# Retention and a gated feed-forward: the fourth block with one key a partition and a DMA transpose

## The chip, the cores and the metric

The kernel runs on one core of a Trainium2 chip. The core has five engines: TensorE (PE in the profile) for matmuls, VectorE (DVE), ScalarE (ACT), GpSimd (POOL), and SyncE (SP), which here only issues DMAs. 16 DMA engines move data between HBM and SBUF, the on-chip memory of 128 partitions; PSUM is the small memory into which TensorE writes. The metric is the device time of one execution in microseconds. Three executions of the kernel before took 296.79, 297.09 and 298.65 us, a median of 297.09. One more was profiled.

## What is computed

The first half is retention, attention without a softmax, with a decay that depends on the head. The second half is a feed-forward layer with the activation h cos(h). q, k and v have 8 batches, 8 heads, 576 positions and 64 columns; in x, the result of the first half, they are 4608 tokens of 512 columns.

```python
scores = q @ k.transpose(0, 1, 3, 2) / sqrt(64)
gamma = 1 - 2.0 ** (-5 - arange(8))                 # one for each head
D = where(rel >= 0, gamma ** rel, 0)                # rel = query position - key position
x = (scores * D) @ v                                # then heads side by side: 4608 x 512
h = x @ w_in                                        # 512 -> 2048
out = (h * cos(h)) @ w_out                          # 2048 -> 512
```

## The kernel before

**Blocks and tiles.** The tokens are cut into 18 blocks of 256 tokens, each of two chunks of 128. Two blocks make a tile of 512 tokens, and there are nine tiles, `n` = 0 to 8. Retention runs by blocks, the feed-forward by tiles, and the blocks of later tiles are worked on between the feed-forward matmuls of the present one.

**A block.** Its steps and their names are as follows.
- `load` brings q, k and v by DMA into float32 tiles `fq`, `fk`, `fv`, three buffers each. The issues stand on the SP queue.
- `scaled` multiplies q and k by powers of gamma that depend on the position and writes them as bf16 into `qks`; `prep` does all four parts on GpSimd. `round_v` casts v into `vb`.
- The transposed q and k, `qkT`, come either from TensorE (`transpose_pe`, with a copy from PSUM) or from one DMA transpose (`transpose_dma`, on the SP queue, named DMA_TRANSPOSE in the profile).
- `scores` multiplies keys and queries inside a chunk into `sc`; VectorE multiplies by a mask into `ret`.
- `sums_of` adds up k times v, the state (`st`), that is carried to later chunks.
- `outputs` adds the chunk's own part (`out_own`, line 375) and the carried part (`out_carried`, line 407) into `ov`, and the result is copied into `xT`.

`qks`, `vb` and `qkT` have four buffers each.

**Two layouts.** A block below `NP_B` (4 before) is in the pair layout: a partition holds two neighbouring keys, 512 contiguous bytes in HBM, and each chunk has half of the partitions. From `NP_B` on, a partition holds one key (two loads each for k and v, in pieces of 256 B), and the state sums and the chunk's own outputs take half the matmuls. q always has two rows a partition. Blocks 0 to 3 are transposed by TensorE, blocks 4 to 17 by DMA.

**The feed-forward.** `mm1` multiplies `xT` by `w_in`; ScalarE takes the cosine (line 457) and VectorE multiplies (line 460) into `gT`. The second matmul of tile 0 is direct (line 927). From tile 1 on `mm2_seven` forms it from seven products (line 563, named x = 1 to 7) of sums of operands, as in Strassen's scheme. The operand sums on the token side (`g_sum`, line 503, tiles `gs3`, `gs5`, `gs6`, `gs7`) are split between VectorE and GpSimd: GpSimd forms gs3 in tile 1 and gs7 in later tiles, four operations each.

**The order.** Nothing is rearranged: each engine executes its instructions in the order of the program text. On the SP queue each DMA is issued behind the one ahead of it, and an issue that must wait holds all that follow. `step` puts `prep`, the DMA transpose and `round_v` of the next block, and a load, in the queues; `steps_to` does so until a given block. In tile 1 the step of block 4 follows the first group of `mm1`, those of 5 and 6 the second, the one of 7 comes behind one of the tile's stores, and the one of 8 in tile 2 behind the seventh group of `mm1`. The scores of block 8 stand in tile 2 inside `mm2_seven`, ahead of product x = 3 (`end_unit`, line 994).

Of the kernel before, what the change touches and what calls it, by code (L numbers as in the profile page):

```python
# [13 lines left out]
ALU = mybir.AluOpType  # L14
# [3 lines left out]
def kernel(  # L18
# [9 lines left out]
    nc = tc.nc  # L28
    P = 128
    B, H, S, D = q.shape  # L30
    assert (B, H, S, D) == (8, 8, 576, 64)
    HG = H // 2
# [14 lines left out]
    last = NT - 1  # L47
    BK = 256
    NB = NTOK // BK
    NP_B = 4  # L50
    PERQ = 9
    PERK = 9
    MIX = PERK // 2
# [131 lines left out]
        tiles["vb", j] = vb  # L185

    def prep(j):
        for name in "kq" if j < NP_B else "qk":
            for y in range(2):
                scaled(nc.gpsimd, j, name, y)  # L190

# [37 lines left out]
    def scores(j, banks):  # L229
        cs = chunks[j]  # L230
        kT = tiles["qkT", j]
        ret = retp.tile([P, 2, HG, 2, P], BF16, tag="ret", name="ret")
        pss = [
            psum.tile([P, HG, 2, P], F32, tag=t, name="sc")
            if isinstance(t, str)
            else [psum.tile([P, HG, P], F32, tag=u, name="sc") for u in t]
            for t in banks
        ]
        if cs[0].pair:
            order = [(c, y, he, hg) for hg in range(HG) for y in range(2) for he in range(2) for c in cs]  # L240
            mask = mask_mix if any(c.mixed for c in cs) else mask_p
            for c, y, he, hg in order:
                ps = pss[he]
                nc.tensor.matmul(
                    ps[y][c.rows, hg, :] if isinstance(ps, list) else ps[c.rows, hg, y, :],
                    lhsT=kT[he * D : he * D + D, 1, y, hg, c.rows],
                    rhs=q_cols(c, he, hg),
                    start=True,
                    stop=True,
                )  # L250

            def masked(he):
                if isinstance(pss[he], list):
                    for y in range(2):
                        nc.vector.tensor_tensor(
                            out=ret[:, he, :, y, :],
                            in0=pss[he][y],
                            in1=mask[:, y].unsqueeze(1).to_broadcast([P, HG, P]),
                            op=ALU.mult,
                        )  # L260
                    return
                nc.vector.tensor_tensor(
                    out=ret[:, he].rearrange("p b r i -> p b (r i)"),
                    in0=pss[he].rearrange("p b r i -> p b (r i)"),
                    in1=mask.rearrange("p r i -> p (r i)").unsqueeze(1).to_broadcast(
                        [P, HG, 2 * P]
                    ),
                    op=ALU.mult,
                )
        else:  # L270
            ret = ret.rearrange("p a b r i -> p (a b r i)").rearrange(
                "p (k a b i) -> p k a b i", k=2, a=2, b=HG
            )
            pss = [
                ps.rearrange("p b r i -> p (b r i)").rearrange("p (a b i) -> p a b i", a=2, b=HG)
                for ps in pss
            ]
            for c in cs:
                for hg in range(HG):
                    for i0 in range(0, P, HP):  # L280
                        for he in range(2):
                            nc.tensor.matmul(  # L282
                                pss[c.k][i0 : i0 + HP, he, hg, :],
                                lhsT=kT[he * D : he * D + D, 1, c.k, hg, i0 : i0 + HP],
                                rhs=q_cols(c, he, hg),
                                start=True,
                                stop=True,
                            )

            def masked(k):  # L290
                mask = mask_cmix if cs[k].mixed else mask_c
                nc.vector.tensor_tensor(  # L292
                    out=ret[:, k].rearrange("p a b i -> p (a b) i"),
                    in0=pss[k].rearrange("p a b i -> p (a b) i"),
                    in1=mask.unsqueeze(1).to_broadcast([P, H, P]),
                    op=ALU.mult,
                )

        tiles["ret", j] = ret
        return [lambda: masked(0), lambda: masked(1)]  # L300
# [213 lines left out]
    def sums_after(n, i):  # L514
        if n == 1:
            slots = {5: ((5, 0, 4),), 6: ((6, 0, 4),)}
        else:
            slots = {
                2: ((7, 0, 4),),
                3: ((5, 0, 4),),  # L520
                4: ((6, 0, 4), (7, 4, 6)),
                5: ((3, 0, 4),),
                6: ((5, 4, 6), (7, 6, E2)),
            }
        for x in slots.get(i, ()):
            g_sum(n, *x)
# [46 lines left out]
    def stored_rows(r0, c0, c1, t, queues=(nc.sync, nc.sync)):  # L573

        rows = out[r0 : r0 + P * t.shape[1], c0:c1].rearrange(
            "(j i r) c -> r i j c", r=2, i=HP
        )
        for r in range(2):
            queues[r].dma_start(rows[r], t[r * HP : (r + 1) * HP])
# [85 lines left out]
    def load_next(**kw):  # L665
        nonlocal loaded
        if loaded < NB:
            load(loaded, **kw)
            loaded += 1
# [143 lines left out]
    w_dma.append(load_w_out(12))  # L813
    scaled(nc.gpsimd, 2, "q", 0)
    load_next(names="kqv", gate=w_dma[6])
    load_next()
    prepared = 4

    def intro(j, sc_banks, st_bank, put_off=None, then=None):
        add = sums_of(j, st_bank)  # L820
# [41 lines left out]

    stores = []

    for n in range(NT):
        blocks = blocks_of.get(n) or [(e + k * E2, 0, W) for e in range(0, E2, 2) for k in range(2)]
        for i, (et, c0, cw) in enumerate(blocks):
            inside = {
                (0, 1): {2: block1_carried},
                (1, 0): {2: lambda: transpose_pe(3, "q", "b", act)},  # L870
                (1, 2): {3: block3_scores},
                (1, 3): {2: lambda: sums_of(3, "st")()()},
            }.get((n, i), {})
            off = [] if (n, i) == (1, 3) else None
            between = block1_sums if (n, i) == (0, 0) else None
            mm1(n, et, c0, cw, banks_of.get(n, "abmabmab")[i], inside, off, between)
            if (n, i) == (0, 0):
                block1_own()
            if (n, i) == (1, 0):
                step(False)  # L880
                load_next()
                for r0, ot in stores:
                    stored_rows(r0, 0, DM, ot)
            if (n, i) == (1, 1):
                step(False)
                load_next()
                step()
            if (n, i) == (1, 3):
                mm2_seven(1, {}, None, (1,), lambda: (outputs(3, "m"), off.pop()()))
            if n:  # L890
                sums_after(n, i)
            if (n, i) == (2, 6):
                step()
        if n == 0:
            gT = tiles["g", n]
            two = psum.tile([P, 2, DM], F32, tag="m", name="o")
# [6 lines left out]
                (37, lambda: round_v(2)),  # L903
                (42, block2_scores),
                (50, block2_sums),
                (50, lambda: prep(3)),
                (57, load_next),
                (59, lambda: round_v(3, (act, act))),
                (60, lambda: outputs(2, "b")),
                (62, lambda: transpose_pe(3, "k", "a", act)),  # L910
            ]
            todo += [
                (at, lambda x=x, e=e: w_sums(x, e, e + 4))
# [10 lines left out]
            for done, (t, e) in enumerate(order):  # L924
                while todo and todo[0][0] <= done:
                    todo.pop(0)[1]()
                nc.tensor.matmul(  # L927
                    pss[t],
                    lhsT=gT[:, e, t * P : (t + 1) * P],
                    rhs=w_out_sb[:, e, :],  # L930
                    start=(e == 0),
                    stop=(e == ET - 1),
                )
                for u in range(2 * (t == 1) if t < 2 else 1) if e == ET - 1 else ():
                    u = u if t < 2 else t
                    ot = op.tile([P, 1, DM], F32, tag="abcd"[u], name="ot")
                    (act, vec)[u % 2](ot[:, 0], pss[u])
                    stores.append((u * P, ot))
            continue

        a, b = 2 * n + 2, 2 * n + 3
# [23 lines left out]
        def first_scores(flush, pend):  # L965
            g_sum(n, 5, 4, E2)
            g_sum(n, 6, 4, E2)
            masks = scores(a, "ab")
            add_a = sums_of(a, "st")
            add_b = sums_of(b, "m")  # L970
            masks[0]()
            add_a()()
            masks[1]()
            g_sum(n, 3, 0, E2)
            g_sum(n, 7, 0, 4)
            tiles["rounded"] = add_b()
            g_sum(n, 7, 4, E2)

        def next_scores(flush, pend):
            outputs(a, "a")  # L980
# [30 lines left out]

        def stored(u):
            if n == 1:
                steps_to({2: 8}.get(u, 0))
            else:
                steps_to({0: 2 * n + 6, 3: 2 * n + 7}.get(u, 0))

# [31 lines left out]
```

## Time and profile before

| | us |
|---|---|
| median of three executions | 297.09 |
| the profiled execution | 296.28 |
| its span, first to last instruction | 294.6 |
| busy: TensorE | 283.2 |
| busy: VectorE | 215.6 |
| busy: GpSimd | 145.6 |
| busy: ScalarE | 143.0 |

The profile is of one execution. Its span is 1.7 us shorter than its device time. Times in the views count from the start of the span. "Busy" is the time in which an engine had an instruction running; waits are given beside it as idle time and what ended it. The chain is followed backwards from the last instruction: at each step to what released it, or to the instruction ahead of it on its engine. An issue on the SP queue (SPq) lasts as long as the queue needs to hand the DMA over, not until the data has landed. The granted clock was 0.994 of full speed on the whole, and below 1 only in the first 12 us.

### The profile page before, as it was taken

To read this page: it belongs to the slowest core of one execution; us is meant where nothing else is said; L and a number is where in the kernel's file an instruction comes from. 1 tells how busy PE (TensorE), PEld (TensorE's weight loads), DVE (VectorE), ACT (ScalarE), POOL (GpSimd) and SP (SyncE) were. 2 spreads that over 40 slices of the span, in tenths; PEclk is the share of its full clock that TensorE was granted. 3 is DMA by queue.
4 is the path that set the end of the run, shared out by engine and by line. 5 is a ranking of instruction groups with operands and counts; after the bars stand their busy time and mean duration, and the time that the engine had idled before them with its cause. 6 is when DMAs were issued, how large, how long until landed. Compare 5 with 4: busy or idle time off the path is not lost.

```text
span 294.6 us, 7623 instructions
## 1 busy us (share of the span) xinstructions
PE 283.2 (96%) x3248; PEld 195.0 (66%) x3268; DVE 215.6 (73%) x268; ACT 143.0 (49%) x166; POOL 145.6 (49%) x172
## 2 busy tenths in 40 slices
PE   7889999999999999999999999999999999999993
PEld 2568755878864688458845884588458845874583
DVE  4585748558986999699659965996599659835933
ACT  4466537646436624563356335633563356326620
POOL 8641535847864495839713961497148014102400
PEclk9799999999999999999999999999999999999999
DMA  7999999999899999999999999979930630121014
GB/s 197 268 222 215 232 247 214 231 181 231 198 199 227 204 240 210 191 219 197 236 203 193 243 215 197 219 128 223 203 64 21 127 71 0 38 65 44 2 37 107
DMA packets 128930, 49.78 MB, mean 169 GB/s; under 512 B 89344, under 2 KB 128384, under 8 KB 128896
## 3 DMA queue, kind: packets, MB, share of 16 engines
q1 hardware_dynamic: 124288, 44.84, 75.6%
q0 software_dynamic: 4224, 4.19, 8.8%
q8 instruction: 25, 0.41, 0.6%
q10 hardware_dynamic: 384, 0.26, 0.4%
q14 instruction: 9, 0.07, 0.1%
HBM read 36.70 MB, written 9.44 MB: 157 GB/s over the span
## 4 chain that ended last, share of the span: by engine, by line
PE 79%; DVE 10%; DMA 4%; POOL 2%; ACT 2%; issue 1%; DVEq 0%; ACTq 0%
PE h L445 38%; PE o L563 27%; PE o L927 5%; DVE gT L460 3%; PE ov L375 3%; DVE gs L503 3%; DMA qkT<-qks 2%; PE st L319 2%; POOL qks L167 2%; PE sc L282 2%; DVE ret L292 2%; PE ov L407 1%; DMA fk<-in_k_dram 1%; PE tr L210 1%; ACT cosh L457 1%
## 5 line engine op out<-in xcount | busy, mean ns | idle before, releaser
L445 PE MATMUL h<-xT,w_in_sb 128*128 128x512 bf16 (+1 forms) x690 | 126.6, 340 | 1.0
L460 DVE TENSOR_TENSOR gT<-h,cosh 128x1024 bf16<-128x1024 f32 x72 | 87.9, 1221 | 37.5 <-ACT cosh L457 37.4
L457 ACT ACTIVATE cosh<-h,half_pi 128x1024 f32<-128x1024 f32 x72 | 80.2, 1114 | 66.4 <-PE h L445 65.1
L445 PEld LDWEIGHTS <-w_in_sb 128*128 128x128 bf16 x704 | 68.4, 98 | 55.3 <-issue 0.6
L503 POOL TENSOR_TENSOR gs<-gT 128x512 bf16<-128x512 bf16 x28 | 35.8, 1280 | 92.2 <-DVE gT L460 92.2
L563 PEld LDWEIGHTS <-gs 128*128 128x128 bf16 x528 | 49.5, 98 | 6.4
L167 POOL TENSOR_TENSOR qks<-fq,gq 128x512 bf16<-128x512 f32 x31 | 33.9, 1113 | 18.1 <-DMA fq<-in_q_dram 14.9
L563 PEld LDWEIGHTS <-gT 128*128 128x128 bf16 x384 | 37.1, 98 | 6.3
L593 ACT COPY ot<-o 128x512 f32<-128x512 f32 x33 | 19.3, 586 | 40.5 <-PE o L563 40.5
L167 POOL TENSOR_TENSOR qks<-fk,gkc 128x512 bf16<-128x512 f32 x28 | 31.8, 1154 | 0.0
L589 DVE TENSOR_TENSOR ot<-ot,o 128x512 f32<-128x512 f32 x35 | 23.2, 680 | 10.9 <-ACT ot L593 7.9
L563 PE MATMUL o<-w_out_sb,gs 128*128 128x256 bf16 (+1 forms) x264 | 30.6, 269 | 0.0
L563 PE MATMUL o<-ws,gs 128*128 128x256 bf16 (+1 forms) x264 | 30.5, 270 | 0.0
L563 PE MATMUL o<-w_out_sb,gT 128*128 128x256 bf16 x256 | 30.5, 273 | 0.0
L292 DVE TENSOR_TENSOR ret<-sc,mask_c 128x1024 bf16<-128x1024 f32 x25 | 29.7, 1214 | 0.1
L430 ACT CAST xT<-ov 128x1024 bf16<-128x1024 f32 x16 | 16.2, 1013 | 11.0 <-PE ov L407 11.0
L178 POOL CAST vb<-fv 128x512 bf16<-128x512 f32 x31 | 18.7, 624 | 5.7 <-DMA fv<-in_v_dram 5.6
L503 DVE TENSOR_TENSOR gs<-gs,gT 128x1024 bf16<-128x1024 bf16 x16 | 15.7, 982 | 0.3
L503 DVE TENSOR_TENSOR gs<-gT 128x512 bf16<-128x512 bf16 (+1 forms) x25 | 15.4, 615 | 0.4
L563 PE MATMUL o<-ws,gT 128*128 128x256 bf16 x128 | 15.3, 273 | 0.0
L349 DVE TENSOR_TENSOR s<-st,s 128x256 f32<-128x256 f32 x18 | 7.6, 421 | 10.4 <-PE st L319 10.1
L359 ACT CAST sb<-s 128x512 bf16<-128x512 f32 (+1 forms) x18 | 10.3, 573 | 9.3 <-DVE s L347 3.8
(81 smaller groups left out, 203.4 us busy)
## 6 DMA issues: line engine op xcount, KB each, us to landing
out_dram<-ot SPq DMA_DIRECT2D x69, 128.0 KB, 2.6
fk<-in_k_dram SPq DMA_DIRECT2D x25, 256.0 KB, 5.7
fv<-in_v_dram SPq DMA_DIRECT2D x25, 256.0 KB, 5.1
fq<-in_q_dram SPq DMA_DIRECT2D x12, 512.0 KB, 5.3
w_in_sb<-in_moe_w_in_dram POOLq DMA_DIRECT2D x4, 512.0 KB, 8.1
w_out_sb<-in_moe_w_out_dram POOLq DMA_DIRECT2D x4, 512.0 KB, 9.8
fk<-in_k_dram SPq DMA_DIRECT2D x3, 512.0 KB, 5.3
fv<-in_v_dram SPq DMA_DIRECT2D x3, 512.0 KB, 7.0
```

What stands on the lines that cost most here:

```text
L167: return eng.tensor_tensor(out=dst.rearrange("p b a d -> p a b d"), in0=src.rearrange("p (a b) d -> p a b d", a=2), in1=by.rearrange("p (a ...
L178: runs[y](vb[:, y], f[:, :, y, :] if j < NP_B else f[:, y])
L292: nc.vector.tensor_tensor(out=ret[:, k].rearrange("p a b i -> p (a b) i"), in0=pss[k].rearrange("p a b i -> p (a b) i"), in1=mask.unsqueez ...
L430: evac(x, ps)
L445: nc.tensor.matmul(ps[:, j, :], lhsT=w_in_sb[:, dg, (et + j) * P : (et + j + 1) * P], rhs=xT[:, dg, c0 : c0 + w], start=(dg == 0), stop=(d ...
L457: nc.scalar.activation(cosh, ps, ACTF.Sin, bias=half_pi, scale=1.0)
L460: nc.vector.tensor_mul(gT[:, et : et + m, c0 : c0 + w], ps, cosh)
L503: i = eng.tensor_tensor(out=tiles["gs", n, x][:, e : e + step], in0=a[:, e : e + step], in1=b[:, e : e + step], op=op_,)
L563: nc.tensor.matmul(dst[i], lhsT=lhs[:, e, j * P : (j + 1) * P], rhs=rhs[:, e, c0:c1], start=(fresh and e == 0 and (i == 0 or len(parts) > 2)),
L589: return lambda: nc.vector.tensor_tensor(out=out_, in0=in0, in1=in1, op=ALU.add)
L593: nc.scalar.copy(t, tiles["all", x])
L927: nc.tensor.matmul(pss[t], lhsT=gT[:, e, t * P : (t + 1) * P], rhs=w_out_sb[:, e, :], start=(e == 0), stop=(e == ET - 1),)
```

## The change

Block 3, the fourth, gets the layout of the later blocks and a DMA transpose, and a few other steps move.
- `NP_B` is 3. `prep(3)` still scales k ahead of q. `scores` learns to use a split pair of PSUM banks in the one-key layout. The gate of block 3's load (on a part of w_out) is now on q alone, since that branch of `load` doesn't use it for k.
- The transposes of block 3 on TensorE are gone; its DMA transpose stands on the SP queue between block 4's k and block 4's v.
- The copy of block 3's outputs is split between ScalarE and VectorE.
- The first tile's stores (eight DMAs), which stood together ahead of block 5's transpose, now follow that transpose (two) and block 6's (six), each with a load behind.
- Block 8's `prep`, transpose and cast are put in the queues at the end of tile 1 instead of late in tile 2. On the SP queue the same DMAs still stand ahead of its transpose, with the new one of block 3.
- On GpSimd, tile 1's gs3 comes after VectorE's gs7 and waits for it, and tile 2's four gs7 operations come together behind block 8's work.

```diff
-    NP_B = 4
+    NP_B = 3
...
-        for name in "kq" if j < NP_B else "qk":
+        for name in "kq" if j <= NP_B else "qk":
...
         if n == 1:
             slots = {5: ((5, 0, 4),), 6: ((6, 0, 4),)}
+        elif n == 2:
+            slots = {3: ((5, 0, 4),), 4: ((6, 0, 4),), 5: ((3, 0, 4),), 6: ((5, 4, 6), (7, 0, E2))}
...
     load_next(names="kqv", gate=w_dma[6])
-    load_next()
-    prepared = 4
+    load(4, "qk")
+    loaded, prepared = 5, 4
...
+    def first_stores(*ts):
+        for t in ts:
+            stored_rows(t * P, 0, DM, stores[t])
...
-                (1, 0): {2: lambda: transpose_pe(3, "q", "b", act)},
...
                 load_next()
-                for r0, ot in stores:
-                    stored_rows(r0, 0, DM, ot)
             if (n, i) == (1, 1):
                 step(False)
+                first_stores(3)
                 load_next()
-                step()
+                step(False)
+                first_stores(0, 1, 2)
+                load_next()
             if (n, i) == (1, 3):
-                mm2_seven(1, {}, None, (1,), lambda: (outputs(3, "m"), off.pop()()))
+                mm2_seven(1, {}, None, (1,), lambda: (outputs(3, "m", act, vec), off.pop()()))
...
-            if (n, i) == (2, 6):
-                step()
...
-                (50, lambda: prep(3)),
+                (50, lambda: (prep(3), transpose_dma(3), load(4, "v"))),
...
-                (62, lambda: transpose_pe(3, "k", "a", act)),
...
-            g_sum(n, 3, 0, E2)
             g_sum(n, 7, 0, 4)
             tiles["rounded"] = add_b()
-            g_sum(n, 7, 4, E2)
+            i = g_sum(n, 7, 4, E2)
+            g_sum(n, 3, 0, E2, gate=i)
...
-                steps_to({2: 8}.get(u, 0))
+                steps_to({2: 8, 3: 9}.get(u, 0))
```

More of the change, by code (lines that the diff above doesn't have):

```diff
@@ L273, in scores @@
             )
+            whole = [
+                None if isinstance(ps, list) else ps.rearrange("p b r i -> p (b r) i") for ps in pss
+            ]
             pss = [
-                ps.rearrange("p b r i -> p (b r i)").rearrange("p (a b i) -> p a b i", a=2, b=HG)
+                ps
+                if isinstance(ps, list)
+                else [
+                    ps[:, he * HG // 2 : (he + 1) * HG // 2].rearrange("p b r i -> p (b r) i")
+                    for he in range(2)
+                ]
                 for ps in pss
@@ L282, in scores @@
                             nc.tensor.matmul(
-                                pss[c.k][i0 : i0 + HP, he, hg, :],
+                                pss[c.k][he][i0 : i0 + HP, hg, :],
                                 lhsT=kT[he * D : he * D + D, 1, c.k, hg, i0 : i0 + HP],
@@ L291, in masked @@
                 mask = mask_cmix if cs[k].mixed else mask_c
[L292 to L297, printed above, removed]
+                if isinstance(banks[k], str):
+                    runs = [(ret[:, k].rearrange("p a b i -> p (a b) i"), whole[k], H)]
+                else:
+                    runs = [(ret[:, k, he], pss[k][he], HG) for he in range(2)]
+                for to, ps, n in runs:
+                    nc.vector.tensor_tensor(
+                        out=to,
+                        in0=ps,
+                        in1=mask.unsqueeze(1).to_broadcast([P, n, P]),
+                        op=ALU.mult,
+                    )
         tiles["ret", j] = ret
@@ L937 @@
                     (act, vec)[u % 2](ot[:, 0], pss[u])
-                    stores.append((u * P, ot))
+                    stores.append(ot)
             continue
```

## The prediction

> **What bounds the kernel.** I read the page's busy shares, its slices and the shares of the chain first:
>
> ```profile
> PE 283.2 (96%) x3248; PEld 195.0 (66%) x3268; DVE 215.6 (73%) x268; ACT 143.0 (49%) x166; POOL 145.6 (49%) x172
> DMA  7999999999899999999999999979930630121014
> PE 79%; DVE 10%; DMA 4%; POOL 2%; ACT 2%; issue 1%; DVEq 0%; ACTq 0%
> ```
>
> TensorE (PE) is busy 283.2 of 294.6 us. At most some 11 us are idle, and about 4 of those lie in the first 20 us, which the change leaves alone. So an edit gains by taking work off TensorE, or loses by making it wait. The DMA row is the second bound: the 16 engines are full from the second slice to the 28th (7.4 us each), that is until about 200 us. A byte added there delays all that follows.
>
> Next comes the chain in order of time (start us, us, what):
>
> ```profile
> 50.95 0.45 PE tr L210 x8
> ...
> 52.70 0.45 PE tr L210 x8
> ...
> 59.49 0.81 PE st L319 x32
> ...
> 62.15 0.35 PE ov L375 x16
> 62.50 0.10 issue
> 62.61 0.42 PE ov L375 x16
> ...
> 102.80 4.64 POOL qks L167 x4
> ...
> 108.92 6.22 DMA qkT<-qks
> 115.14 0.04 issue
> 115.19 0.64 PE sc L282 x32
> ...
> 133.24 0.37 PE st L319 x16
> 133.61 0.45 PE ov L375 x16
> ```
>
> The rows at 50 to 63 us are block 3. The rows at 133 us are the same work for a block with one key a partition. At 115.19 us TensorE has waited for block 8's DMA transpose (0.22 us, by the waits): the only DMA wait of the span after the start, so there is no room left at this place. The chain lays the transpose to GpSimd's scaling of block 8. The SP queue's own rows say otherwise:
>
> ```profile
> 44.16 3.56 SPq L149 DMA_DIRECT2D fk<-in_k_dram  x2
> 47.83 3.13 SPq L149 DMA_DIRECT2D fv<-in_v_dram  x2
> ...
> 97.59 2.27 SPq L197 DMA_TRANSPOSE qkT<-qks  x1
> 99.90 0.72 SPq L135 DMA_DIRECT2D fq<-in_q_dram  x1
> 100.68 1.86 SPq L149 DMA_DIRECT2D fk<-in_k_dram  x2
> 102.59 2.56 SPq L149 DMA_DIRECT2D fv<-in_v_dram  x2
> 105.25 3.56 SPq L579 DMA_DIRECT2D out_dram<-ot  x4
> 108.92 3.10 SPq L197 DMA_TRANSPOSE qkT<-qks  x1
> ```
>
> Each issue starts about 0.1 us after the one before it ends, and so it goes from 38.15 to 130 us (one pause of 0.6 us). GpSimd ends block 8's k at 102.80 + 4.64 = 107.44, but the four stores ahead hold the queue until 108.81. The queue came last. [...]
>
> **TensorE's work.** The 16 PE transposes of block 3 go: 2 x 0.45 = 0.90 us. Its state sums fall from 32 to 16 matmuls, 0.81 to 0.37: 0.44 us. Its own outputs fall from 32 with a drain to 16: 0.35 + 0.10 + 0.42 - 0.45 = 0.42 us. The scores stay 32 matmuls. Together **1.76 us**, all on the path, since TensorE is hardly ever idle there. ScalarE loses two 1.03 us evacuations, which lie beside matmuls: nothing. Block 3's output copy is split between ScalarE and VectorE: TensorE idled 0.13 us before 64.47, so at most 0.1 us. VectorE adds two state sums (0.42 each) in place of one (0.68): beside matmuls, nothing. TensorE comes to block 8's scores at 114.97 - 1.8 = **113.2 us**.
>
> **The SP queue.** One transpose (block 3's) is added between block 4's k and v. The trace has 14, whose issue holds the queue 1.57 to 3.56 us; the six from 58 to 121 us took 3.56, 2.27, 3.26, 2.27, 3.10 and 2.15, mean 2.77. Block 3's v becomes two loads of 256 B pieces: 3.13 us (47.83) against 2.33 for the one at 39.25, so +0.8. Its k becomes two loads too, and loses its wait for w_out, because the one-key branch of `load` never uses the gate. It can issue from 31.07 us, where the queue now stands idle until 38.15: -0.4 of issue, and its bytes can fill a dip of the DMA at 36 to 38 us (149 GB/s against 231 before it), worth up to 0.7. The small terms nearly cancel, so I take the transpose alone, **+2.7 us** for everything behind. Bounds: +1.6 (shortest issue, v paid for by k) and +4.4 (longest issue, v in full). The eight stores of the first tile move behind block 5's and block 6's transposes; all still stand ahead of block 8's, so there the count is the same: nothing.
>
> **Where it is hidden.** Block 3's own transpose issues at about 47.8 us (k's issue ends 47.72, GpSimd's q ends 47.56) and lands 4.4 to 6.9 us later (all 14 do; median 5.1), by 54.7. Its scores stand at 57.01 - 0.9 = 56.1: hidden with 1.4 us to spare. If that cover goes, the wait only uses up the saving before block 8 does. Block 5's is issued at 74.88 now; without 5.8 us of stores ahead and with 2.7 more, at 71.8, landing 76.2 to 78.7 against a need at 80.55 - 1.8 = 78.75: just hidden. Block 7's: 97.59 + 2.7, landing by 107.2, needed at 109.5: hidden.
>
> **Block 8.** Issue 108.92 + 2.7 = 111.6, landing 5.1 later at **116.7** (bounds 108.92 + 1.6 + 4.4 = 114.9 and 108.92 + 4.4 + 6.9 = 120.2). TensorE waits from 113.2 to 116.7, 3.5 us, and resumes 1.5 us later than now. The saving is inside this: it only lengthens the wait. Behind the waiting matmul stand the product x = 3 and the whole of the next tile. From there to the end TensorE is 99% busy, so nothing is won back.
>
> **GpSimd's sums.** In tile 2 gs7 (4 x 1.28 us) goes behind block 8's scaling and casts, which can then end at about 103 us (its v issues until 93.75 + 2.7, lands 5.1 later, casts 1.2); the queue still holds the transpose, so this alone buys nothing. gs7 then ends at about 108.1, needed pair by pair from 106.7 to 108.0: hidden, or it eats into the wait. In tile 1 gs3 starts only when VectorE ends gs7, about 80.1, and takes 4 x 1.36 = 5.4 us: to 85.5, where the product wants its last quarter at about 84.5. A wait of 1.0 us, but ahead of the 3.5 us one, so free. VectorE's two sums at 75 to 80 us (1.53 and 1.60 beside gs3, 0.69 alone) get 1.7 us shorter. TensorE waits 0.6 us in all there, so at most 0.6, and swallowed too.
>
> **The clock.** Stretches of 3.41 us (busy us per engine, granted clock, DMA share, GB/s):
>
> ```profile
> 5.06:8.47 3.41, 1.97 (x18) 0.94 (x17) 2.68 (x4) 1.50 (x3) 3.13 (x5) 1.00 1.16 290
> 8.47:11.89 3.42, 3.42 (x71) 2.26 (x70) 1.56 (x2) 1.58 (x4) 1.26 (x2) 0.50 1.18 279
> 288.35:291.76 3.41, 1.70 (x24) 1.45 (x21) 1.24 (x5) 0.00 (x0) 0.00 (x0) 1.00 0.75 182
> ```
>
> A stretch with TensorE busy 1.97 us, in sparse pieces, was followed by 3.4 us at half clock. At the end one with 1.70 us of dense matmuls was not followed by it. A wait of 3.5 us leaves one stretch idle for about 1.8 us or more however the stretches fall. I take one stretch at half clock: 3.41 / 2 = **+1.7 us** (bounds 0 and 3.4, a second stretch).
>
> [...]
>
> **Sum.** 294.6 + 1.5 + 1.7 = 297.8 us of span. The profiled execution took 296.28, 1.7 more than its span: 299.5. The median of the runs shown (297.09) is 0.8 above the profiled one, so a median of **300.3 us**.
>
> **Rivals**, on the median's scale.
> - *No clock loss*: the wait comes, but no stretch is idle enough, as in the last row above. 297.09 + 1.5 = 298.6. Chance 0.20.
> - *The queue absorbs the transpose* (the other side: not slower). The decider is block 8's issue at 113.2 - 4.4 = 108.8 or earlier. For it: k's early issue, and stores in two groups that may fill gaps after the transposes (DMA share 0.95 in 70 to 90 us). Against: 83 us of queue with one pause. Then 1.8 us are saved: 295.3; with all of TensorE's idle time from 36 to 116 us too (1.9), 293.4. Chance 0.18.
> - *Later still*: the transpose lands near its upper bound, 2 us after my value. 302.4. Chance 0.12.
> - *GpSimd is late instead*: block 8 lands in time, but gs3's 1.0 us is paid: 296.3. Chance 0.05.
>
> The forecast has 0.45. A measurement tells 1% (3.0 us: 294.1 to 300.1) from no change. Slower by more: two thirds of the forecast, all of "later still", a quarter of "no clock loss": 0.47. Faster by more: under half of the absorbing case: 0.08. The rest, 0.45, is within 1%. The range 295.0 to 302.5 leaves out the top of the bounds and the best case.
>
> **What would show it.** The profile after should have a wait of 2.5 to 5 us of TensorE for the DMA transpose of block 8 at 113 to 117 us, a slice of PEclk below 9 or a stretch at 0.50 just behind it, an SP queue without pauses from 38 us, and block 8's scaling done long before its transpose issues. No PE transposes after 45 us, and n = 3 onward as before, only shifted. I am wrong if that transpose issues before 109 us, if TensorE's wait there is under 1 us, or if the clock stays full behind a wait over 3 us.

## The result

The changed kernel took 303.94 to 306.14 us in four executions, median **305.84 us**, against 296.94 us for the kernel before in the same measurement. The ratio is **1.0275**, 95% interval 1.0217 to 1.0333: slower. I had forecast 300.3 us, with a range up to 302.5. Medians here are of all executions; the ratios below leave out three, one of e2 and two of e7, that took over 1.5% longer than the fastest of their kernel. The profiled execution took 303.94 us, the shortest of the four, so the profile shows the change at its mildest: its span is 302.2 us, 7.6 more than before (294.6).

The page of the changed kernel has these rows for the busy shares, the 40 slices and the shares of the chain:

```profile
PE 285.0 (94%) x3220; PEld 194.3 (64%) x3220; DVE 217.8 (72%) x270; ACT 140.5 (46%) x164; POOL 146.0 (48%) x172
PE   6899999989989993999999999999999999999993
PEclk9799999999999999799999999999999999999999
DMA  7999999999999999999899999997960630022014
PE 76%; DVE 8%; DMA 5%; POOL 4%; ACT 2%; SPq 2%; issue 1%; DVEq 0%; POOLq 0%; ACTq 0%
```

TensorE is busy 1.8 us *more* (285.0 against 283.2), although it has less work. One slice, the 16th (113.3 to 120.9 us), is busy for only three tenths, and in the 17th the granted clock falls to 0.7. The DMA engines stay full for about as long as before.

The list of TensorE's waits names what emptied that slice (total us, times, longest):

```profile
PE sc L290 <- DMA qkT<-qks: 5.5, 2, 5.3
```

TensorE's timeline of the changed kernel (start, duration, what, and in brackets the idle time before it) shows where they stand:

```profile
56.91 0.64 PE L290 MATMUL sc<-qkT 64*64 64x128 bf16 x32 [0.20 <-DMA qkT<-qks]
...
62.81 0.36 PE L420 MATMUL ov<-qkT,sb 64*64 64x128 bf16 x12 [0.66 <-ACT sb L372]
...
86.73 0.61 PE L578 MATMUL o<-w_out_sb,gs 128*128 128x256 bf16 x4 [0.65 <-POOL gs L516]
...
121.47 1.07 PE L290 MATMUL sc<-qkT 64*64 64x128 bf16 x32 [5.30 <-DMA qkT<-qks]
122.47 2.84 PE L578 MATMUL o<-w_out_sb,gs 128*128 128x256 bf16 x16
```

The kernel before, the same scores:

```profile
115.19 0.64 PE L282 MATMUL sc<-qkT 64*64 64x128 bf16 x32 [0.22 <-DMA qkT<-qks]
```

The wait for block 8's transpose, 0.22 us before, is 5.30 us. The scores behind it take 1.07 us instead of 0.64: they run at half clock. The stretches of 3.41 us show the same (busy time of PE, PEld, DVE, ACT, POOL, granted clock, DMA share, GB/s):

```profile
114.15:117.56 3.41, 2.02 (x48) 1.46 (x46) 3.32 (x6) 1.47 (x3) 1.92 (x3) 1.00 0.79 180
117.56:120.97 3.41, 0.00 (x0) 0.00 (x0) 0.00 (x0) 0.00 (x0) 0.00 (x0) 1.00 1.17 146
120.97:124.39 3.42, 2.92 (x42) 2.20 (x43) 2.23 (x2) 0.00 (x0) 0.17 (x1) 0.50 1.03 238
```

The SP queue of the changed kernel (start, time that the queue is held, what) answers to the one shown of before:

```profile
48.98 4.46 SPq L197 DMA_TRANSPOSE qkT<-qks  x1
53.53 1.15 SPq L149 DMA_DIRECT2D fv<-in_v_dram  x2
...
61.68 4.48 SPq L197 DMA_TRANSPOSE qkT<-qks  x1
...
73.56 3.81 SPq L197 DMA_TRANSPOSE qkT<-qks  x1
...
84.11 4.78 SPq L197 DMA_TRANSPOSE qkT<-qks  x1
88.93 3.79 SPq L594 DMA_DIRECT2D out_dram<-ot  x6
...
111.13 4.71 SPq L594 DMA_DIRECT2D out_dram<-ot  x4
115.95 3.45 SPq L197 DMA_TRANSPOSE qkT<-qks  x1
```

Block 8's transpose issues at 115.95 us (108.92 before, 111.6 forecast) and lands at 121.42. The two at 73.56 and 84.11, blocks 5 and 6, hold the queue 3.81 and 4.78 us; before they held it 2.27 and 3.26.

TensorE's start differs by up to 0.9 us between the profiles: block 2's scores stand at 43.88 us before, 44.01 after, 43.77 in e9 below, and 43.07 to 43.35 in the other experiments. The three late ones have a stretch at half clock at 8 to 12 us. So TensorE's path is counted from there. The SP queue doesn't share this shift: block 4's k, behind the same DMAs in these three, is issued at 44.16 us before, 44.07 in e4 and 43.97 in e3, where TensorE is 0.7 us earlier. Its times are counted from the start of the span.

The span then divides as follows: TensorE comes to block 8's scores 1.07 us later than before (72.16 against 71.09 us behind block 2's scores), waits 5.08 longer, and loses 1.7 at half clock (3.42 / 2). With 0.13 us of later start that is 8.0; behind it 0.4 us come back.

### The profile page after: what moved, and what is told of

Same layout as the page of the kernel before. It is cut to its first block, busy times and chain, and to the rows that moved or that the text cites. A ratio compares the mean times of both kernels' runs of the same rounds, so it can differ in the third digit from the quotient of the medians.

```text
span 302.2 us, 7548 instructions
## 1 busy us (share of the span) xinstructions
PE 285.0 (94%) x3220; PEld 194.3 (64%) x3220; DVE 217.8 (72%) x270; ACT 140.5 (46%) x164; POOL 146.0 (48%) x172
## 4 chain that ended last, share of the span: by engine, by line
PE 76%; DVE 8%; DMA 5%; POOL 4%; ACT 2%; SPq 2%; issue 1%; DVEq 0%; POOLq 0%; ACTq 0%
PE h L458 38%; PE o L578 26%; PE o L943 4%; PE ov L388 2%; DMA fv<-in_v_dram 2%; DVE gT L473 2%; DMA qkT<-qks 2%; POOL gs L516 2%; PE sc L290 2%; DVE gs L516 2%; DVE ret L305 2%; PE st L332 2%; POOL qks L167 1%; DMA fk<-in_k_dram 1%; PE ov L420 1%
## 5 line engine op out<-in xcount | busy, mean ns | idle before, releaser
L167 POOL TENSOR_TENSOR qks<-fq,gq 128x512 bf16<-128x512 f32 x31 | 34.7, 1140 | 28.1 <-DMA fq<-in_q_dram 22.1
L305 DVE TENSOR_TENSOR ret<-sc,mask_c 128x1024 bf16<-128x1024 f32 (+1 forms) x28 | 32.1, 1176 | 4.8 <-PE sc L290 4.7
L167 POOL TENSOR_TENSOR qks<-fk,gkc 128x512 bf16<-128x512 f32 x30 | 33.3, 1129 | 1.8 <-DMA fk<-in_k_dram 1.8
L578 PE MATMUL o<-w_out_sb,gs 128*128 128x256 bf16 (+1 forms) x264 | 31.7, 274 | 0.7 <-POOL gs L516 0.7
L443 ACT CAST xT<-ov 128x1024 bf16<-128x1024 f32 x15 | 15.2, 1013 | 9.6 <-PE ov L420 9.6
L362 DVE TENSOR_TENSOR s<-st,s 128x256 f32<-128x256 f32 x20 | 8.4, 421 | 9.7 <-PE st L332 9.4
L290 PE MATMUL sc<-qkT 64*64 64x128 bf16 x480 | 9.8, 223 | 5.5 <-DMA qkT<-qks 5.5
```

What stands on the lines that cost most here:

```text
L167: return eng.tensor_tensor(out=dst.rearrange("p b a d -> p a b d"), in0=src.rearrange("p (a b) d -> p a b d", a=2), in1=by.rearrange("p (a ...
L290: nc.tensor.matmul(pss[c.k][he][i0 : i0 + HP, hg, :], lhsT=kT[he * D : he * D + D, 1, c.k, hg, i0 : i0 + HP], rhs=q_cols(c, he, hg), start ...
L305: nc.vector.tensor_tensor(out=to, in0=ps, in1=mask.unsqueeze(1).to_broadcast([P, n, P]), op=ALU.mult,)
L443: evac(x, ps)
L578: nc.tensor.matmul(dst[i], lhsT=lhs[:, e, j * P : (j + 1) * P], rhs=rhs[:, e, c0:c1], start=(fresh and e == 0 and (i == 0 or len(parts) > 2)),
```

## The experiments

Three questions were open: which part of the change makes block 8's transpose late, where TensorE's 1.76 us went, and what half clock is worth. All kernels compute the whole result.

**e2: all of the change except block 3's DMA transpose.** Block 3 has the new layout, but TensorE transposes it.

```diff
-    load(4, "qk")
-    loaded, prepared = 5, 4
+    load_next()
+    prepared = 4
...
+                (1, 0): {2: lambda: transpose_pe(3, "q", "b", act)},
...
-                (50, lambda: (prep(3), transpose_dma(3), load(4, "v"))),
+                (50, lambda: prep(3)),
...
+                (62, lambda: transpose_pe(3, "k", "a", act)),
```

> The changed kernel, but block 3, still one key a partition, is transposed by TensorE as before; no transpose of it on the SP queue. Theory S: block 8's transpose lands some 3.5 us earlier, about 118, so a wait of 2 us stays; no half clock; 300 to 302 us. Theory Q: the wait is gone, 296 to 297 us. If TensorE's saving were real, one would see it arrive at block 8's scores earlier than the 114.97 us of the kernel before, by about 0.8; if it is eaten by VectorE's and ScalarE's state sums, at 115 or later.

Measured: 298.00 us, ratio 1.0042 (1.0012 to 1.0071). Without this one DMA the kernel is 7.8 us faster by the medians than with it (2.3%, or 6.9 us, by the ratios). Block 8's transpose in e2, in the SP queue and in TensorE's timeline:

```profile
111.97 2.69 SPq L197 DMA_TRANSPOSE qkT<-qks  x1
...
116.70 0.64 PE L290 MATMUL sc<-qkT 64*64 64x128 bf16 x32 [0.40 <-DMA qkT<-qks]
```

The wait is 0.40 us, and half clock is gone. Yet TensorE arrives at 116.30, that is 73.1 us behind block 2's scores, where the kernel before needed 71.1. It has 0.86 us less work there and comes 2 us later. So a second loss stands on TensorE's own path, which the wait in the full change covers.

**e9: e2 with plain loads of the same size in place of the transpose.** Two loads of 256 KB in 256 B pieces, whose data nobody reads, stand where block 3's transpose stood.

```diff
-                (50, lambda: (prep(3), transpose_dma(3), load(4, "v"))),
+                (50, lambda: (prep(3), same_bytes(), load(4, "v"))),
...
+    def same_bytes():
+        extra = sump.tile([P, 2, H, D], F32, tag="gs7", name="extra")
+        for y in range(2):
+            s0 = y * P
+            nc.sync.dma_start(extra[:, y], v[3, :, s0 : s0 + P, :].rearrange("h s d -> s h d"))
```

> The kernel of e2 (block 3 transposed by TensorE) with two plain loads of 256 KB in pieces of 256 B on the SP queue where block 3's DMA transpose stands in the changed kernel; what they bring is not used. They are as many packets (2048) as the transpose's. If a transpose costs what its bytes cost, block 8's transpose lands at 121 us as in the changed kernel and the time is 304 to 306. If the transpose costs more by draining the engines, it lands about 2.3 us behind e2's 116.7, at 119: 300.5 to 302.5 us.

Measured: 303.68 us, ratio 1.0251 (1.0200 to 1.0303), with a wait of 2.87 us for block 8. Against e2 (116.66 us) the bytes alone put off the landing by 3.4 us (120.07), the transpose by 4.8 (121.42). So 3.4 us of the 4.8 came with two plain loads of that size as well. The other 1.4 us may be the transpose itself, but two profiles of the same queue order (the change and e5, below) differ by more.

**e4: the kernel before with the two groups of stores alone.**

```diff
-                for r0, ot in stores:
-                    stored_rows(r0, 0, DM, ot)
             if (n, i) == (1, 1):
                 step(False)
+                for r0, ot in stores[3:]:
+                    stored_rows(r0, 0, DM, ot)
                 load_next()
-                step()
+                step(False)
+                for r0, ot in stores[:3]:
+                    stored_rows(r0, 0, DM, ot)
+                load_next()
```

> The kernel before with the two groups of stores alone (two behind block 5's transpose, six behind block 6's). Theory S: block 5's transpose holds the queue about 1.5 us longer, and the stores behind a transpose leave the DMA engines short of work, so block 8's lands 2.5 to 3.5 us later than 115.14: 300 to 301.5 us. Theory Q: 297 us, as before.

Measured: 299.63 us, ratio 1.0106 (1.0056 to 1.0157). I had costed this part at nothing. Its SP queue, at blocks 5 and 6:

```profile
68.32 4.68 SPq L197 DMA_TRANSPOSE qkT<-qks  x1
73.10 1.18 SPq L579 DMA_DIRECT2D out_dram<-ot  x2
...
79.95 4.55 SPq L197 DMA_TRANSPOSE qkT<-qks  x1
84.55 5.13 SPq L579 DMA_DIRECT2D out_dram<-ot  x6
```

The kernel before, the same two transposes:

```profile
68.96 5.81 SPq L579 DMA_DIRECT2D out_dram<-ot  x8
74.88 2.27 SPq L197 DMA_TRANSPOSE qkT<-qks  x1
...
84.42 3.26 SPq L197 DMA_TRANSPOSE qkT<-qks  x1
```

The eight stores take about as long (5.8 us in one group, 6.3 in two), but the transposes hold the queue 9.2 us together instead of 5.5. Block 8's transpose then issues 2.2 us later than before (111.15 against 108.92), so part of the 3.7 us is made up on the way. TensorE arrives at block 8 exactly as before (71.1 us behind block 2's scores) and waits 2.09 us. After that wait the clock is halved, as the stretches of e4 show (columns as above):

```profile
114.25:116.34 2.09, 0.01 (x2) 0.00 (x0) 1.31 (x3) 1.32 (x2) 0.00 (x0) 1.00 0.98 223
116.34:117.20 0.86, 0.85 (x35) 0.74 (x36) 0.39 (x1) 0.00 (x0) 0.00 (x0) 1.00 0.76 197
117.20:120.60 3.40, 3.40 (x18) 2.31 (x16) 2.28 (x3) 0.00 (x0) 1.43 (x2) 0.50 1.30 262
```

**e1: the change with the stores back in one group ahead of block 5's transpose.**

```diff
                 step(False)
                 load_next()
+                first_stores(0, 1, 2, 3)
             if (n, i) == (1, 1):
                 step(False)
-                first_stores(3)
                 load_next()
                 step(False)
-                first_stores(0, 1, 2)
                 load_next()
```

> The changed kernel with the first tile's eight stores put back in front of block 5's transpose. Theory S (half of the delay of block 8's transpose comes from the order: a transpose issued straight behind loads holds the SP queue 3.3 to 4.8 us, one behind stores 2.2 to 3.1): block 5's issue falls from 3.8 to about 2.3 us, block 8's transpose lands about 3 us earlier than the changed kernel's 121.4, the time falls by about 3 us to 303. Theory Q (the order is free, block 3's added transpose is all): within 0.6 us of the changed kernel, 305.8.

Measured: 303.61 us, ratio 1.0201 (1.0150 to 1.0253). The expectation that block 8's transpose would come some 3 us earlier failed: it issued 1.3 us earlier than in the full change (114.67 against 115.95) and landed only 0.7 us earlier (120.72 against 121.42). With the stores ahead of it, block 5's transpose issues at 80.70 and TensorE waits for it instead (TensorE's timeline of e1):

```profile
85.25 1.07 PE L290 MATMUL sc<-qkT 64*64 64x128 bf16 x32 [3.42 <-DMA qkT<-qks]
```

Two stretches at half clock follow (84.5 to 91.4 us). So the two groups do keep block 5's transpose in time, as the prediction had it; they only move the wait to block 8.

**e5: the change with 16 matmuls of zeros, into a bank that nobody reads, ahead of block 8's scores.**

```diff
             def then():
                 flush()
                 outputs(b, "m")
+                if n == 2:
+                    warm(16, "n")
```

> The changed kernel with 16 matmuls of zeros (3.4 us, 128 x 512) on TensorE just ahead of block 8's scores, into a bank that is free there. They lie inside the 5.3 us wait. If the 1.3 to 1.7 us behind the wait are the half clock, the granted clock stays 1.0 there and the time falls by 1.3 to 1.7 us to about 304.3. If they are something else, the time stays at 305.8 or rises.

Measured: 303.78 us, ratio 1.0216 (1.0171 to 1.0260), 2.1 us below the change, though the intervals overlap. TensorE's timeline of e5:

```profile
118.44 3.63 PE L220 MATMUL idle<-zeros 128*128 128x512 bf16 x16
123.44 0.64 PE L290 MATMUL sc<-qkT 64*64 64x128 bf16 x32 [1.37 <-DMA qkT<-qks]
```

The scores take 0.64 us again, at full clock. The medians agree with the 1.7 us at which one stretch at half clock was priced.

This profile also shows how far two executions of one queue order lie apart. Up to block 8's scores e5's order is that of the change, yet block 8's transpose issues at 118.00 us, 2.05 later. Block 3's transpose was late too: TensorE waited 1.52 us for it, against 0.20 in the profile of the change. In e1 and e6 it waited 1.67 and 1.27. And at 52.60 us TensorE waited 1.74 us for ScalarE's copy of block 2's outputs (0.22 in the change). That copy stands behind ScalarE's cast of block 3's v, which waited 1.42 us for v's load. The profile of the change is of its fastest execution; that its other three lost their 1.9 us at block 3 is likely, but was only argued, since no profile shows them.

**e6: the change with tile 1's stores behind block 8's transpose.**

```diff
+                if n == 1:
+                    stored(s)
                 stored_rows(n * W + r * 256, c * N2, (c + 1) * N2, t, queues)
-                stored(s)
+                if n != 1:
+                    stored(s)
...
-                steps_to({2: 8, 3: 9}.get(u, 0))
+                steps_to({1: 9}.get(u, 0))
```

> The changed kernel with tile 1's eight stores behind block 8's transpose on the SP queue (they stood ahead of block 7's and 8's). The DMA engines took about 2.3 us for four stores, so block 8's transpose should land up to 4.6 us earlier, less what two transposes straight behind loads cost more (about 1.5 us each): 118 to 120 us against 121.4, a wait of 2 to 4 us, 302 to 304.5 us. If the stores ran free in gaps: 121.4 and 305.8.

Measured: 301.65 us, ratio 1.0166 (1.0122 to 1.0209). Block 8's transpose issues 5.6 us earlier (110.32 us, 115.95 in the change) and TensorE doesn't wait for it. But the eight stores now stand behind it, and block 10's transpose is late instead (TensorE's timeline of e6):

```profile
148.39 0.64 PE L290 MATMUL sc<-qkT 64*64 64x128 bf16 x32 [3.01 <-DMA qkT<-qks]
```

A wait of 3.01 us, this time with no loss of clock at all: the scores take 0.64 us. Here, too, moving a transfer forward moved the wait to another block.

**e3: the kernel before with GpSimd's order alone** (block 8's `prep`, transpose and cast at the end of tile 1, gs3 behind gs7, tile 2's sums rearranged).

```diff
+        elif n == 2:
+            slots = {3: ((5, 0, 4),), 4: ((6, 0, 4),), 5: ((3, 0, 4),), 6: ((5, 4, 6), (7, 0, E2))}
...
-            if (n, i) == (2, 6):
-                step()
...
-            g_sum(n, 3, 0, E2)
             g_sum(n, 7, 0, 4)
             tiles["rounded"] = add_b()
-            g_sum(n, 7, 4, E2)
+            i = g_sum(n, 7, 4, E2)
+            g_sum(n, 3, 0, E2, gate=i)
...
-                steps_to({2: 8}.get(u, 0))
+                steps_to({2: 8, 3: 9}.get(u, 0))
```

> The kernel before with GpSimd's new order alone (gs3 of tile 1 behind VectorE's gs7, gs7 of tile 2 together, block 8 prepared at the end of tile 1). If the SP queue holds block 8's transpose, as the prediction said, it still lands at 115 +- 1 us, though GpSimd has block 8 ready some 5 us earlier. TensorE waits 0.7 us for gs3 and so comes to block 8's scores later than 114.97: 297 to 298 us. If GpSimd held the transpose: it lands by 113 and the time falls by 0.2 us or more.

Measured: 296.39 us, ratio 1.0023 (0.9992 to 1.0055): no difference. The profiled execution was a long one (299.0 us) with a wait of 1.95 us for VectorE's `gT` at 103 us and half clock behind it. Block 8's transpose landed at 112.95 us, 2.2 earlier than before (115.14), where I had expected that only if GpSimd held it. But the queue held it here too: the stores ahead end at 107.59 and it issues at 107.70. The queue was already 1.0 us ahead at blocks 6 and 7; why is not shown.

**e7: the kernel before with block 3's new layout and the split output copy**, TensorE still transposing.

```diff
-    NP_B = 4
+    NP_B = 3
...
-                mm2_seven(1, {}, None, (1,), lambda: (outputs(3, "m"), off.pop()()))
+                mm2_seven(1, {}, None, (1,), lambda: (outputs(3, "m", act, vec), off.pop()()))
```

> The kernel before with block 3 in the one-key layout and its output copy split, transposed by TensorE; stores and GpSimd as before. TensorE has 0.86 us less to do (0.44 sums, 0.42 outputs). Theory P (the state's path VectorE, ScalarE, TensorE sets the pace at 57 to 64 us, and two state sums are 0.16 us longer there than one): it comes to block 8's scores no earlier than 114.9, 297 us. If the work counts, it comes at 114.1 and the time is 296 to 296.3, unless block 8's transpose holds it.

Measured: 298.18 us, ratio 1.0065 (1.0034 to 1.0096): slower, with 0.86 us less work for TensorE. Its timeline of TensorE shows where that went:

```profile
62.50 0.36 PE L420 MATMUL ov<-qkT,sb 64*64 64x128 bf16 x12 [0.66 <-ACT sb L372]
...
64.28 6.93 PE L458 MATMUL h<-xT,w_in_sb 128*128 128x256 bf16 x62 [0.22 <-DVE xT L446]
...
77.33 2.79 PE L576 MATMUL o<-ws,gs 128*128 128x256 bf16 x24 [0.44 <-DVE gs L516]
...
81.92 0.42 PE L290 MATMUL sc<-qkT 64*64 64x128 bf16 x16 [0.61 <-DVE s L362]
```

The first wait stands right behind the saving. TensorE reaches block 3's carried outputs sooner, but the state that they need comes from VectorE's two sums (0.88 us together, one of 0.68 before) and ScalarE's copy, and these are no sooner. The last two waits are for VectorE, whose operand sums became slower; 0.38 us of the last stands in the kernel before too. Together the four are 1.55 us longer than before. TensorE comes 1.3 us later with 0.86 us less work, so some 0.6 us stand in no listed wait. The kernel before, VectorE's sums at 70 to 76 us:

```profile
70.57 0.69 DVE L503 TENSOR_TENSOR gs<-gT 128x1024 bf16<-128x1024 bf16 x1
...
72.31 0.95 DVE L503 TENSOR_TENSOR gs<-gs,gT 128x1024 bf16<-128x1024 bf16 x1
...
74.43 0.69 DVE L503 TENSOR_TENSOR gs<-gT 128x1024 bf16<-128x1024 bf16 x1
```

The same three in e7:

```profile
70.16 0.85 DVE L516 TENSOR_TENSOR gs<-gT 128x1024 bf16<-128x1024 bf16 x1
...
72.07 1.40 DVE L516 TENSOR_TENSOR gs<-gs,gT 128x1024 bf16<-128x1024 bf16 x1
...
74.63 1.08 DVE L516 TENSOR_TENSOR gs<-gT 128x1024 bf16<-128x1024 bf16 x1
```

Together they take 1.0 us more. GpSimd's scaling of block 6, which waits for q's load, started at 67.64 us before and at 68.42 in e7 (1.5 us later from block 2's scores), so other steps of GpSimd lie beside them. A sum of the same shape took 0.68 us with GpSimd idle (at 81.19 us, before), and 0.69 (70.57) to 1.60 (78.88) while it worked. That GpSimd made them slower is my reading; it was not tried alone.

**e10: e7 with the output copy whole on ScalarE again.**

```diff
-                mm2_seven(1, {}, None, (1,), lambda: (outputs(3, "m", act, vec), off.pop()()))
+                mm2_seven(1, {}, None, (1,), lambda: (outputs(3, "m"), off.pop()()))
```

> The kernel before with block 3 in the one-key layout, as in e7, but its output copy whole on ScalarE again (one cast of 1.01 us in place of 0.59 and 0.69 on two engines). e7 came to block 8's scores 72.4 us behind block 2's scores (43.15 to 115.56), the kernel before 71.1 (43.88 to 114.97), although e7 has 0.86 us less work for TensorE there. Theory 'small waits': the saving was eaten by four waits of e7, of which only the one of 0.22 us for VectorE's half of the copy belongs to the split. The others are 0.66 us behind ScalarE's copy of the state, which stays since VectorE still makes two state sums of 0.44 us instead of one of 0.68, and 0.44 and 0.61 us behind VectorE's operand sums, which took 0.85, 1.40 and 1.08 us beside GpSimd instead of 0.69, 0.95 and 0.69, since GpSimd's scaling of block 6 lay 0.8 us later. Then the 0.66 us wait is there, and the distance is 71.9 to 72.4 us; median 0 to 0.3 us below e7's 298.2, never below the kernel before by 0.5. Theory 'split copy': the split keeps VectorE busy and makes all of the later waits; then the distance falls to 70.5 or less and the median is 0.8 us or more below e7's, that is below the kernel before on the same chip.

Measured: 296.97 us, ratio 1.0032 (1.0011 to 1.0052). The wait of 0.22 us is gone and that of 0.66 stays. The two for VectorE's sums are now 0.78 and 0.76 us, and TensorE reaches block 8's scores 72.6 us behind block 2's, no sooner than e7. So the split copy isn't the cause of the later waits. On the distance the theory of small waits comes closest, 0.2 us off its range. On the time it doesn't fit: e10's ratio is 0.33% below e7's, about 1 us, at the edge of what the intervals tell apart, where at most 0.3 us was expected. e7's profile can't show that excess, since it is of the fastest of its ten executions (296.80 us).

**e11: e10 with block 8's `prep`, transpose and cast early**, GpSimd's order otherwise as before.

```diff
-            if (n, i) == (2, 6):
-                step()
...
-                steps_to({2: 8}.get(u, 0))
+                steps_to({2: 8, 3: 9}.get(u, 0))
```

> e10 with block 8's scaling, transpose and cast put in the queues at the end of tile 1 (as in the change), the rest of GpSimd's order as before. Theory 'queue': block 8's transpose is held by the SP queue alone, so it issues and lands as in e10 (about 110 and 115.7 us) and the time is the same within 0.3 us. Theory 'scaling': in e3 this order went with a landing at 112.9 instead of 115.1 us, since GpSimd's scaling (103 to 108 us in e7) was the later condition; then the transpose lands at 112.5 to 114 us, TensorE has no wait for it at block 8, and the median is 0.2 to 0.6 us below e10's. A price that could turn it: tile 2's gs7 (four sums, 1.2 to 1.5 us each) now stands behind the scaling of block 8 and the product that wants it at about 107 us waits for GpSimd; a wait over 0.5 us there would undo the gain.

Measured: 298.17 us, ratio 1.0071 (1.0051 to 1.0091), 1.2 us slower than e10. The transpose issued at 109.97 (109.86 in e10) and landed at 115.18 (115.48): the queue alone holds it, not the scaling. The price was not the one I had named, a late gs7. The scaling now runs at 94 to 98 us beside VectorE's sums of tile 2, and gs7 behind it as one block of 5.13 us. VectorE's sums there take 0.99, 1.08 and 1.35 us (0.69, 0.68 and 0.41 in e10), and its products `gT` come late (TensorE's timeline of e11):

```profile
103.42 1.92 PE L576 MATMUL o<-w_out_sb,gT 128*128 128x256 bf16 x16 [0.28 <-DVE gT L473]
105.83 0.61 PE L576 MATMUL o<-w_out_sb,gT 128*128 128x256 bf16 x4 [0.49 <-DVE gT L473]
```

No version here beats the kernel before; e3 alone is level with it.

**The parts side by side**, each from one profile. The transpose is given in us from the start of the span, TensorE's arrival in us behind block 2's scores:

```
                               transpose of block 8     TensorE at
                               issued       landed      block 8's scores
before                         108.92       115.14       71.1
e7   layout, split copy        110.06       115.72       72.4
e4   two store groups          111.15       116.30       71.1
e3   GpSimd's order            107.70       112.95       74.6 (1.7 of it half clock)
e2   all but the transpose     111.97       116.66       73.1
e9   e2 + the same bytes       113.89       120.07       73.5
after                          115.95       121.42       72.2
e5   after + 16 matmuls        118.00       123.39       75.1 (ahead of the 16)
```

## Why the prediction was wrong

The mechanism was right: block 8's transpose is late on a full SP queue, TensorE waits, half clock follows, and nothing is won back. TensorE was forecast to resume 1.5 us later than before; it resumed 6.15 later. Two terms of the sum were mis-sized.

1. **"Together 1.76 us, all on the path": failed.** TensorE came to block 8's scores 1.1 us later, not 1.8 earlier. e7 shows that the layout's 0.86 us are lost without any DMA transpose. The 0.90 us of the transposes seem to have come: the change arrives 1.0 us sooner than e2, where TensorE still transposes block 3 (72.2 against 73.1). "TensorE is hardly ever idle there" was no reason to count a saving as earliness: behind block 3's state sums stands a chain over VectorE and ScalarE, which had no slack and got 0.2 us longer. "VectorE adds two state sums: beside matmuls, nothing" failed with it (0.66 us of wait in e2, e7 and e10). Part of the rest went to VectorE's sums, slower in e7 while GpSimd worked (1.40 us at 72.07 us, against 0.68 for a sum of the same shape in the change at 79.52, with GpSimd idle), and some 0.6 us of e7's loss is not located.

2. **The queue, "+2.7 us for everything behind": failed as a sum, not in its first term.** Block 8's transpose issued 7.0 us later (115.95 against 108.92) and landed at 121.42 instead of the forecast 116.7. The added transpose is 4.0 us of the 7.0 (the change against e2), inside the bounds of 1.6 to 4.4; with e5's profile in place of the change's it would be 6.0, outside them. What failed are the two terms put at nothing. "All still stand ahead of block 8's, so there the count is the same: nothing" was wrong by +2.2 us (e4): the count is the same, but block 5's transpose, now behind loads instead of stores, held the queue 4.68 us instead of 2.27, and block 6's, behind loads in both, 4.55 instead of 3.26. "The small terms nearly cancel" was wrong by about +1 us (1.1 in e7, 0.9 in e10): v's two loads held the queue 4.59 us instead of 2.33, where I had 0.8 us more, and k's early issue didn't bring v forward (39.45 us in e7, 39.25 before). In e3 the queue ran 1.2 us ahead. The parts add up to 6.1, against 7.0 measured together. But they need not add: taking the store groups out of the full change (e1) gave back 1.3 us, not 2.2. And with 2.05 us between two profiles of the same order, the sizes are estimates, while the times of e2 and e4 show that both parts cost. That block 8's early prep "alone buys nothing" was right (e11).

3. **Hidden or not.** Block 5's transpose landed at 79.64 us for scores at 80.81, and block 7's 4.9 us ahead of its scores: hidden, as forecast. Block 3's was not "hidden with 1.4 us to spare": it landed at 56.86, not by 54.7, and cost 0.20 us. It issued 1.2 us later than forecast and took 7.9 us to land, more than any of before; it stands straight behind k's two loads.

4. **GpSimd.** The wait for gs3 came, 0.65 us for a forecast of 1.0, and it was swallowed. "At most 0.6" of gain from VectorE's lighter load was none: the four sums at 72 to 81 us took 4.60 us instead of 4.77, and block 6's scaling slid beside the first three (71.84 to 76.77 us).

5. **The clock: right.** One stretch at half clock, 1.7 us; e5 gives 2.1 by medians, with intervals that overlap. In the change the 3.41 us ahead of it (117.56 to 120.97) were empty; in e4 half clock came behind a wait of 2.09 us.

The rival of an absorbing queue (295.3) is ruled out by the issue time alone, and "later still" (302.4) was the right direction and too small: its upper bound for the landing, 120.2 us, was passed by 1.2.

## What to carry to other kernels

On this full DMA queue the neighbours of a transposing DMA counted, not only how many transfers stood ahead: regrouping stores, with the number unchanged, put a later transpose off by 2.2 us and cost about 3 us of time (e4). A saving of TensorE work ahead of a chain over other engines was worth nothing here (0.86 us less work in e7, and an arrival 1.3 us later), so find what TensorE will wait for next before you count it. Where every part is a little late, take the parts one at a time: here the layout and the store groups each cost something alone, and the full change hid which.

## What the runs showed of the hardware

**The issue of a transpose ended about when the transfer ahead of it landed.** In the table below, from the DMA records of the changed kernel, the issue of each transpose ends within 0.6 us of the landing of the DMAs ahead of it; over all 29 transposes of both kernels the difference lies between -0.6 and +0.9 us, with a median of about 0.2. From 36 to 130 us loads landed a median of 4.2 (before) and 4.6 us (after) behind the end of their own issue, stores 3.0 and 2.0. In the two profiles a transpose straight behind loads held the queue 3.3 to 4.8 us, and behind stores 1.6 to 3.7. Whether the issue waits for that landing was not tried.

```
            issue starts   issue ends   ahead landed   lands    ahead
block 3        48.98         53.43         53.64       56.86    loads
block 4        61.68         66.17         66.51       68.17    loads
block 5        73.56         77.38         77.96       79.64    loads
block 6        84.11         88.88         89.02       90.70    loads
block 7       103.10        105.41        104.99      107.61    stores
block 8       115.95        119.41        119.62      121.42    stores
```

**Which waits were followed by half clock.** One stretch of 3.4 us at half clock followed waits of 1.95 (e3), 2.09 (e4), 2.87 (e9) and 5.30 us (the change), and two followed one of 3.42 (e1). None followed a wait of 3.01 us in e6. In the profile of the change the granted clock falls at 8.33 and at 120.97 us and is back 3.41 us later each time; the two falls lie 112.64 us apart, 33 times 3.413. So I laid the waits over stretches of that length. The last ones ahead of half clock in e3 and e4, then the two that share e6's wait (columns as above):

```profile
101.03:104.44 3.41, 1.47 (x14) 1.16 (x13) 3.41 (x4) 1.20 (x2) 1.65 (x3) 1.00 1.17 262
113.82:117.23 3.41, 1.32 (x55) 1.03 (x52) 2.16 (x5) 1.32 (x2) 0.00 (x0) 1.00 0.81 191
143.23:146.64 3.41, 2.15 (x51) 1.61 (x48) 1.44 (x3) 1.79 (x3) 1.00 (x2) 1.00 0.95 199
146.64:150.06 3.42, 1.67 (x42) 1.47 (x43) 1.20 (x2) 0.33 (x1) 0.00 (x0) 1.00 0.97 224
```

Where TensorE was busy for 1.47 us (e3), 1.32 (e4), about 0.7 (e1, ahead of 84.5 us) and 0.00 (the change) of a stretch at full clock, the next one came at half clock. Behind 2.15 and 1.67 us (e6), and 2.02 in the change (114.15 to 117.56), it came at full clock. e6's wait was cut by a border at 146.64 us into 1.26 and 1.75 us. So in these a wait that kept TensorE idle for 1.94 us or more of one such stretch was followed by half clock, and one of 1.75 us was not. In the first 12 us, where the work comes in sparse pieces, stretches with TensorE busy for 1.97 us (before) and 1.87 (the change, 4.92 to 8.33) were followed by half clock too. These limits are those of these stretches alone, and what the clock counts stays open.
